# Seven-product matmuls whose running sums move from bank to bank of PSUM by ScalarE copies

## The chip, the core and the metric

The kernel runs on one core of a Trainium2 chip. The core has a matrix engine (TensorE, PE in the profile, with weight loads as PEld), a vector engine (VectorE, DVE), an activation engine (ScalarE, ACT), a general engine (GpSimd, POOL) and SyncE (SP), which issues most transfers. Matmul results go to PSUM, eight banks of 128 partitions by 512 fp32 values; everything else lies in SBUF. Each engine works through its own queue in order and waits on semaphores for the others. The metric is the device time of one execution in microseconds, from first to last instruction and what lies around them; lower is better.

## The reference, cut to what matters

The first part is a linear attention over 8 batches, 8 heads, 576 positions, 64 channels; its output becomes x of shape 4608 x 512. The change does not touch it. The second part routes all tokens through all eight experts, weighted:

```
x = attention output                      # (4608, 512)
P = sinkhorn(exp(x @ w_gate))             # (4608, 8), 8 rounds of normalising
for e in range(8):
    h = max(x @ w1[e], 0)                 # (4608, 512) @ (512, 1024)
    out += P[:, e:e+1] * (h @ w2[e])      # (4608, 1024) @ (1024, 512)
```

## The kernel before, in words

The tokens are cut into nine groups of 512 (group 8 holds the last 64 positions of each batch). Attention comes first, with expert 0's up matmuls filled in; routing and expert 0's down matmuls follow. From there on, experts 1 to 7 are computed with seven products in place of eight (a Strassen-Winograd scheme): both operands are seen as 2 x 2 blocks, VectorE makes sums and differences of blocks (`sub`, the line 1199 in the profile), and seven block products are combined into four result blocks.

*Up* (`up7`). One call treats two groups of 512 tokens at a time (pairs 0-1, 2-3, 4-5, 6-7, in two halves of the hidden width) or group 8 alone: nine calls per expert, 63 in all. In each call every product is made twice, for q = 0 and 1, each into a bank of its own. The products are named x1, x2, x3, x4, y1, w1, w2. The x products accumulate one after the other in bank x, w1 and w2 in bank w, y1 stands alone in bank y. Between them the running sum is read out:

- x1, then `keep`: ScalarE copies x to an SBUF tile U (line 1360). y1, then `add`: VectorE adds y and U, applies the relu and writes hidden block (1,1) (line 1364).
- x2 on top of x1, `keep` into a second U. x3 on top, `keep` into the first U; `add` of w (holding w1) and U gives block (0,0).
- x4 on top, `relu` by ScalarE (line 1369) gives block (0,1).
- w2 on top of w1, `add` of w and the second U gives block (1,0).

*Down* (`down7`) has the products X1, Y1, Z1, X2, X3, Z2, X4 of 8 matmuls each, in banks x, y and z, for one group of 512 tokens. `read` (line 1501) is two VectorE instructions that scale half a bank by the routing weight P and add it to the output accumulator. `read2` does the same by two ScalarE activations into an SBUF tile V (line 1513) and one GpSimd add onto the accumulator (line 1516). X1, Y1, Z1 and X3 end in `read2`, X2, Z2 and X4 in `read`. X1 and Y1 both belong to block (0,0) and are added to it one after the other. There are 62 such down sets.

Matmuls of 512 columns are line 1316 (`wide`, up of a pair), of 256 columns line 1307 (`product`, group 8's up and all downs). Each up set is issued together with the down set of an earlier group, in the order

`X1 x10 w10 x11 X2 x20 y10 x21 Z1 y11 X3 w11 x30 x31 x40 x41 w20 Y1 w21 X4 Z2`

where the digit at the end is q. This list is not yet the order on the chip. Every operation is handed to a planner (`Plan`), which keeps a cost for each operation, the dependencies, and the free PSUM banks (`Banks`, one shared set of eight; `P1` takes one bank, `P2` two). It lays the operations out in its own time: it always takes the one that can start first, on ties the one that comes earlier in the list, and emits each engine's instructions in that order. So a change of dependencies or of bank use moves the matmuls against each other. Expert weights are loaded by DMAs that GpSimd issues (line 476), the precombined blocks of x by DMAs from SyncE (line 1274). A matmul with `start=True` overwrites its bank, one with `start=False` adds to what stands there.

In the attention part VectorE also rewrites a bank in place between two sets of accumulating matmuls (line 872 between matmuls of line 864).

Of the kernel before, what the change touches and what calls it, by code (L numbers as in the profile page):

```python
# [69 lines left out]
class Banks:  # L70


    def __init__(self, tile, free, n):
        self.psum, self.free, self.n = True, free, n
        self.make = lambda i: tile[:, 512 * i:512 * (i + n)]

    def pick(self):

        if self.n == 1:
            order = sorted((t, i ^ 1 in self.free, i) for i, t in self.free.items())  # L80
            return (order[0][0], order[0][2]) if order else None
        order = sorted((max(self.free[i], self.free[i + 1]), i) for i in range(0, 8, 2)
                       if i in self.free and i + 1 in self.free)
        return order[0] if order else None

    def find(self, n):
        if n == 1:
            best = self.pick()
            return best and best[0]
        assert self.n == 1  # L90
        return sorted(self.free.values())[n - 1] if len(self.free) >= n else None

    def take(self, at):
        i = self.pick()[1]
        if self.n == 1:
            i = min((k ^ 1 in self.free, -t, -k, k) for k, t in self.free.items() if t <= at)[3]
        for k in range(self.n):
            del self.free[i + k]
        return i

    def give(self, end, slot):
# [215 lines left out]
def kernel(  # L317
# [11 lines left out]
    nc = tc.nc  # L329
# [130 lines left out]
    ring("s_p", [128, 3, E], FP32, "cs", 1)  # L460
    ring("s_p", [128, E], FP32, "c_bc", 1)
    banks = {i: 0.0 for i in range(8)}
    R["P1"], R["P2"] = Banks(ps, banks, 1), Banks(ps, banks, 2)

    def new(tag):
        return R[tag].new()
# [116 lines left out]
    def two(merged):  # L583

        if merged:
            b = new("P2")
            return [b], [lambda: b()[:, 0:512], lambda: b()[:, 512:1024]]
        b = [new("P1") for _ in range(2)]
        return b, b

    def tokens(pp, stat, n, r, takes=()):
# [35 lines left out]
    def rest_a(b, t):  # L627
# [4 lines left out]
        if b >= 2:  # L632
            rk = [(t["qk"], h, x) for h in range(2) for x in range(2)]
        if b < 2:
            ptr = new("P1")
            for pr in range(NP):
                pe(128, lambda pr=pr: nc.tensor.transpose(
                    ptr()[:, pr * 128:pr * 128 + 128],
                    acc[0][:, b, pr * 128:pr * 128 + 128], identf),
                    [("acc", 0, b, h, x) for h in range(2) for x in range(2)] + ["identf"],  # L640
                    [ptr, ("acc", 0, b)])
            dve(512, lambda: nc.vector.tensor_copy(
                out=rT().rearrange("p a b -> p (a b)"), in_=ptr()), [ptr], [rT])
        else:
            dma("SP", 1 << 17, 148, lambda: nc.sync.dma_start_transpose(
                out=rT(), in_=t["qk"]()[:, bi:bi + NP].rearrange("p a b c -> p (a b c)")),
                rk, [rT])
# [53 lines left out]
    def pair_a(b, pr, t):  # L701
# [3 lines left out]
        if b < 2:  # L705
            g = t["f"]
            for x in (1, 0):
                ptr = new("P1")
# [118 lines left out]
    def pair_b(b, pr, s, r):  # L827
# [4 lines left out]
        pkv = new("P1")  # L832

        def kvp(x):
            return pkv()[:, 0:4 * D1].rearrange("p (a b) -> p a b", a=2)[:, x, :]
# [18 lines left out]
        xb = new("xb")  # L854

        def outs(h):
            pn = new("P1")
# [27 lines left out]
    def pair_c(b, pr, xb):  # L885
        if b in (3, 4, 5, 6,):
# [4 lines left out]
        pxt = new("P1")  # L891
        for j in range(NJ):
            pe(128, lambda j=j: nc.tensor.transpose(  # L893
                bf(pxt)[:, j * 128:j * 128 + 128], xb()[:, j, :], ident),
# [3 lines left out]
            [pxt], [("xT", b, pr)])  # L898

    def rest_c(b, xbs):  # L900
        pxt = new("P1")
# [14 lines left out]
        return [("xTr", b, h) for b in range(B) for h in range(2)]  # L916

    def gate(g):
        pg = new("P1")
        for ti in range(4):  # L920
            for dc in range(NP):
                pe(8, lambda ti=ti, dc=dc: mm(
# [182 lines left out]
    def routing():  # L1105
        c_bc = None
        for it in range(8):
            rr, wv, cs, pc = new("rr"), new("T"), new("cs"), new("P1")
            lk = [("L", g) for g in range(NG)]
            if c_bc is None:  # L1110
                def u():
# [209 lines left out]
    def up7(A, gs, fp, X, H, r0):  # L1321


        pair = len(gs) == 2
# [5 lines left out]
                    "t4": (lambda: X[4](), [X[4]])}[n]  # L1330
            return f, r

        x, y, w = ([new("P1") for _ in range(2)] for _ in range(3))
        u = [[new("U") for _ in range(2)] for _ in range(2)]
        hb = [H[g][fp] for g in gs] if pair else H[gs[0]]

        def prod(bank, q, x, y, first, more=(), takes=(), wk=()):
# [18 lines left out]
        def okeys(q, i, j):  # L1356
            return [(z, q, i, j) for z in hb] if pair else [(hb[q], n, i, j) for n in range(2)]

        def keep(q, n):
            act(512, lambda: nc.scalar.copy(  # L1360
                out=u[q][n]().rearrange("p a b -> p (a b)"), in_=x[q]()), [x[q]], [u[q][n]])

        def add(bank, q, n, i, j):
            dve(515, lambda: nc.vector._custom_dve(  # L1364
                ADD_SAT, out=out_(q, i, j), in0=bank[q]().rearrange("p (a b) -> p a b", a=2),
                in1=u[q][n](), s0=3.0e38, s1=0.0), [bank[q], u[q][n]], okeys(q, i, j))

        def relu(q, i, j):
            act(512, lambda: nc.scalar.activation(  # L1369
                out=out_(q, i, j), in_=x[q]().rearrange("p (a b) -> p a b", a=2),  # L1370
                func=ACT.Relu, bias=0.0, scale=1.0), [x[q]], okeys(q, i, j))


        more = [("banks", 0), ("banks", 1)]
        more += [k for n in ("s2", "s3", "22") for k in A[n][1]] + [X[2]] + list(r0)

        def x1(q):
            prod(x, q, "11", "11", True, more, u[q] + hb)
            keep(q, 0)

        def y1(q):
            prod(y, q, "12", "21", True, r0, hb)
            add(y, q, 0, 1, 1)

        def x2(q):
            prod(x, q, "s2", "t2", False)
            keep(q, 1)

        def w1(q):
            prod(w, q, "s1", "t1", True, A["s4"][1] + r0, hb, [("banks", q)])  # L1390

        def x3(q):
            prod(x, q, "s3", "t3", False)
            keep(q, 0)
            add(w, q, 0, 0, 0)

        def x4(q):
            prod(x, q, "22", "t4", False)
            relu(q, 0, 1)

        def w2(q):
            prod(w, q, "s4", "22", False)
            add(w, q, 1, 1, 0)

        return {(n, q): lambda f=f, q=q: f(q) for n, f in (
            ("x1", x1), ("y1", y1), ("x2", x2), ("w1", w1), ("x3", x3), ("x4", x4), ("w2", w2))
# [5 lines left out]
    def down8(e, g, H, w2):  # L1412

        def tile_(ts, n0, n):
            py = new("P1")
# [25 lines left out]
    def down7(e, g, H, B7):  # L1441
# [79 lines left out]
        if e == 1 and g < 9:  # L1521
            for ts in range(4):
# [1 line left out]
                    out=acc[g][:, ts, :], in_=acc[g][:, ts, :], func=ACT.Copy, bias=0.0,  # L1524
                    scale=P[:, 4 * g + ts, 0:1]), ["P", ("acc", g, ts), (H[0], 0, 1, 1)] + akey(g),
                    [("acc", g, ts, j) for j in range(2)])
        x, y, z = new("P1"), new("P1"), new("P1")

        def X1():
            prod(x, a(0, 0), "11", hk(0, 0), True, sk(1) + hk(1, 0),  # L1530
                 [("D", e, g)])
            read2(x, 0, 0)

        def Y1():
            prod(y, a(0, 1), "21", hk(0, 1), True, [("D", e, g)])
            read2(y, 0, 0)

        def Z1():
# [116 lines left out]
```

## Time and profile before

| what | value |
|---|---|
| time, median of 3 runs (lowest, highest) | 1023.16 us (1022.22, 1023.96) |
| span of the profiled execution, first to last instruction | 1020.7 us |
| PE busy, matmuls | 1007.1 us (99%), 7944 |
| PEld busy | 686.1 us (67%) |
| DVE busy | 853.2 us (84%), 1833 instructions |
| ACT busy | 701.6 us (69%), 1530 instructions |
| POOL busy | 466.8 us (46%), 480 instructions |
| granted TensorE clock | 1.000 |
| chain that ended last | PE 95%, ACT 2%, DVE 1% |

The page gives no time of the profiled execution other than its span; the median of the runs is 2.5 us above that span.

How to read the lines that follow: a group line has the kernel line, the engine, the operation, output<-input by the program's names, the shapes, the count, then busy microseconds, mean nanoseconds of one, and the idle time of the engine just before these instructions with what ended it. A waits line reads "who <- for whom: us in total, times, longest". A timeline line reads start, duration, engine, line, operation and the number of instructions merged into it; a merged line covers from the first start to the last end. A matmul's recorded time includes its way through the array, so the spacing of starts, not the recorded duration, tells how dense TensorE is.

### The profile page before, as it was taken

The numbers are of one execution on the slowest core, as the hardware profiler recorded it, in microseconds if no ns is written. First come the engines' busy times: TensorE is split into PE (matmuls) and PEld (weight loads), VectorE is DVE, ScalarE is ACT, GpSimd is POOL, SyncE is SP. The second block draws the span as 40 slices with busy tenths as digits, with TensorE's granted clock in tenths as the row PEclk, the third lists the DMA queues.
The fourth block names the chain that finished last, engine by engine and source line by source line (L and its number), as shares of the span: only waits on it lengthen the run. The fifth ranks groups of instructions, "written<-read, shape, count | busy, mean of one in ns | idle before, by whom it ended". The sixth has DMA issues, their size and how long they took to land.

```text
span 1020.7 us, 21372 instructions
## 1 busy us (share of the span) xinstructions
PE 1007.1 (99%) x7944; PEld 686.1 (67%) x7944; DVE 853.2 (84%) x1833; ACT 701.6 (69%) x1530; POOL 466.8 (46%) x480
## 2 busy tenths in 40 slices
PE   7899999999999999999999999999999999999998
PEld 5666666644566766676667766676667666776665
DVE  7999989987888987788778887788778877888776
ACT  7999999836778665666666666556666666655663
POOL 5778764400244444444444444544444444544443
PEclk9999999999999999999999999999999999999999
DMA  9999988160103311161106111421125110612333
GB/s 264 174 194 175 174 149 126 36 114 11 42 32 69 82 32 32 27 135 32 32 27 114 33 42 37 82 54 32 31 47 115 32 32 26 109 43 73 129 124 130
DMA packets 107016, 82.86 MB, mean 81 GB/s; under 512 B 53536, under 2 KB 89376, under 8 KB 106912
## 3 DMA queue, kind: packets, MB, share of 16 engines
q1 hardware_dynamic: 74960, 57.44, 22.4%
q0 software_dynamic: 31648, 23.86, 16.9%
q8 instruction: 62, 1.02, 0.4%
q14 instruction: 42, 0.34, 0.1%
q10 hardware_dynamic: 304, 0.20, 0.1%
HBM read 83.18 MB, written 12.98 MB: 94 GB/s over the span
## 4 chain that ended last, share of the span: by engine, by line
PE 95%; ACT 2%; DVE 1%; issue 0%; POOL 0%; DMA 0%; DVEq 0%; ACTq 0%
PE ps L1307 41%; PE ps L1316 33%; PE ps L581 18%; PE ps L864 2%; PE ps L711 0%; ACT q L577 0%; DVE m L573 0%; ACT k L577 0%; DVE wx L573 0%; DMA acc<-in_k_dram 0%; PE ps L893 0%; ACT kr L577 0%; ACT wx L577 0%; DVE xb L878 0%; PE ps L903 0%
## 5 line engine op out<-in xcount | busy, mean ns | idle before, releaser
L1516 POOL TENSOR_TENSOR acc<-acc,hx 128x512 f32<-128x512 f32 x248 | 322.9, 1309 | 476.7 <-ACT hx L1513 473.3
L1360 ACT COPY U<-ps 128x512 f32<-128x512 f32 x378 | 216.6, 588 | 134.1 <-PE ps L1316 117.6
L1513 ACT ACTIVATE hx<-ps,P 128x256 f32<-128x256 f32 x496 | 208.0, 476 | 124.6 <-PE ps L1307 112.0
L1364 DVE CUSTOM_DVE_ANT_0 hs<-ps,U 128x512 bf16<-128x512 f32 x378 | 253.0, 687 | 35.7 <-PE ps L1316 15.0
L1307 PEld LDWEIGHTS <-hs 128*128 128x128 bf16 x1984 | 194.1, 98 | 72.8 <-issue 0.2
L1501 DVE SCALAR_TENSOR_TENSOR acc<-ps,P,acc 128x256 f32<-128x256 f32 x372 | 161.2, 478 | 92.3 <-PE ps L1307 91.5
L1307 PEld LDWEIGHTS <-hx 128*128 128x128 bf16 x1488 | 145.6, 98 | 40.0 <-issue 0.2
L1307 PE MATMUL ps<-hx,hs 128*128 128x256 bf16 x992 | 132.5, 273 | 0.0
L1316 PE MATMUL ps<-X,T 128*128 128x512 bf16 x448 | 129.0, 379 | 0.3 <-ACT U L1360 0.2
L1316 PE MATMUL ps<-xT,wx 128*128 128x512 bf16 x384 | 101.5, 379 | 0.0
L1316 PEld LDWEIGHTS <-T 128*128 128x128 bf16 x672 | 65.8, 98 | 48.0 <-issue 0.3
L1369 ACT ACTIVATE hs<-ps 128x512 bf16<-128x512 f32 x126 | 73.2, 609 | 12.3 <-PE ps L1316 12.3
L1307 PE MATMUL ps<-wx,hs 128*128 128x256 bf16 x560 | 80.4, 273 | 0.0
L1316 PEld LDWEIGHTS <-wx 128*128 128x128 bf16 x512 | 50.1, 98 | 38.4 <-issue 0.5
L1316 PE MATMUL ps<-xT,w 128*128 128x512 bf16 x288 | 75.6, 379 | 0.0
L581 PE MATMUL ps<-w,hx 128*128 128x512 bf16 x288 | 73.7, 379 | 0.0
L581 PE MATMUL ps<-xT,w 128*128 128x512 bf16 x288 | 72.9, 379 | 0.0
L1307 PE MATMUL ps<-wx,hx 128*128 128x256 bf16 x496 | 68.4, 273 | 0.0
L1316 PE MATMUL ps<-xT,T 128*128 128x512 bf16 x224 | 66.0, 379 | 0.0
L1307 PE MATMUL ps<-hx 128*128 128x256 bf16 x496 | 64.3, 273 | 0.1
L1199 DVE TENSOR_TENSOR hx<-hx,hs 128x512 bf16<-128x512 bf16 x124 | 64.2, 518 | 0.0
L1307 PE MATMUL ps<-w,hs 128*128 128x256 bf16 x432 | 62.7, 273 | 0.0
(147 smaller groups left out, 1516.2 us busy)
## 6 DMA issues: line engine op xcount, KB each, us to landing
X<-xd SPq DMA_DIRECT2D x72, 256.0 KB, 2.6
wx<-in_moe_w_dram POOLq DMA_DIRECT2D x8, 1024.0 KB, 12.5
v_m<-in_v_dram SPq DMA_DIRECT2D x15, 512.0 KB, 5.3
out_dram<-acc SPq DMA_DIRECT2D x14, 512.0 KB, 2.8
w<-in_moe_w_dram POOLq DMA_DIRECT2D x6, 1024.0 KB, 12.0
qk<-in_k_dram POOLq DMA_DIRECT2D x12, 256.0 KB, 5.5
qk<-in_q_dram POOLq DMA_DIRECT2D x12, 256.0 KB, 6.3
xd<-X SPq DMA_DIRECT2D x12, 256.0 KB, 2.1
```

The lines of the kernel that those rows point to most:

```text
L581: nc.tensor.matmul(out_, lhsT=lhsT, rhs=rhs, start=start, stop=stop)
L864: pe(65, lambda j=j: nc.tensor.matmul(pn()[:, j * D1:j * D1 + D1], lhsT=s["T"][x]()[:, j % 2, 2 * h + j // 2, :] if j < 4 else r["T"][x]() ...
L1199: lambda: f.tensor_tensor(out=out_(), in0=x(), in1=y(), op=op), r, w, **kw)
L1307: pe(256, lambda i=i, k=k, z=z: nc.tensor.matmul(bank()[:, 256 * i:256 * i + 256], lhsT=lhs(k, i), rhs=rhs(k), start=first and z, stop=k = ...
L1316: pe(512, lambda k=k: nc.tensor.matmul(bank().rearrange("p (a b) -> p a b", a=2), lhsT=lhs(k), rhs=rhs(k), start=first and k == 0, stop=k ...
L1360: act(512, lambda: nc.scalar.copy(out=u[q][n]().rearrange("p a b -> p (a b)"), in_=x[q]()), [x[q]], [u[q][n]])
L1364: dve(515, lambda: nc.vector._custom_dve(ADD_SAT, out=out_(q, i, j), in0=bank[q]().rearrange("p (a b) -> p a b", a=2), in1=u[q][n](), s0=3 ...
L1369: act(512, lambda: nc.scalar.activation(out=out_(q, i, j), in_=x[q]().rearrange("p (a b) -> p a b", a=2), func=ACT.Relu, bias=0.0, scale=1 ...
L1501: dve(320, lambda n=n, ts=ts: nc.vector.scalar_tensor_tensor(out=acc[g][:, ts, 256 * j:256 * j + 256], in0=bank()[:, 256 * n:256 * n + 256 ...
L1513: act(370, lambda n=n: nc.scalar.activation(out=u()[:, n, :], in_=bank()[:, 256 * n:256 * n + 256], func=ACT.Copy, bias=0.0, scale=P[:, 4 ...
L1516: pool(695, lambda: nc.gpsimd.tensor_tensor(out=acc[g][:, 2 * i:2 * i + 2, 256 * j:256 * j + 256], in0=acc[g][:, 2 * i:2 * i + 2, 256 * j: ...
```

## The change

In `up7` the running sums move inside PSUM. After x1, ScalarE copies bank x into bank y (`move`), and y1 accumulates on top of it, so bank y then holds the sum and ScalarE's relu writes block (1,1). After x2, ScalarE copies bank x into a new bank z, and w2 accumulates there. w1 is copied to U by ScalarE (`keep`) and its bank is given back. x3's sum in bank x and U are added by VectorE to block (0,0), and z and U to block (1,0). x4 is as before. Per q, ScalarE goes from three copies and one relu to three copies (two of them into PSUM) and two relus, VectorE from three adds to two.

In `down7`, X1 is copied by ScalarE from bank x to bank y, Y1 accumulates on top, and one `read2` takes the sum to block (0,0), where there were two.

The planner's banks get kinds: `whole` for a bank whose 512 columns are all written by the first matmuls, `part` for others, and `onto` for a bank that is first written by a copy; `onto` takes only banks whose last matmuls wrote all of it. `P1` is `whole`, the new `PP` is `part` (the attention, gate, routing and last down tiles use it), the new `PO` is `onto`. The order list is unchanged.

```diff
 class Banks:
+    def usable(self):
+        return [(i, t) for i, t in self.free.items() if self.kind != "onto" or i in self.whole]
...
         for k in range(self.n):
             del self.free[i + k]
+            (self.whole.discard if self.kind == "part" else self.whole.add)(i + k)
...
-    R["P1"], R["P2"] = Banks(ps, banks, 1), Banks(ps, banks, 2)
+    whole = set()
+    for tag, n, kind in (("P1", 1, "whole"), ("P2", 2, "part"), ("PP", 1, "part"),
+                         ("PO", 1, "onto")):
+        R[tag] = Banks(ps, banks, n, whole, kind)
...
-        x, y, w = ([new("P1") for _ in range(2)] for _ in range(3))
-        u = [[new("U") for _ in range(2)] for _ in range(2)]
+        x, w = ([new("PO" if q == 0 and t in inner else "P1") for q in range(2)]
+                for t in ("11", "s1"))
+        y, z = ([new("PO") for _ in range(2)] for _ in range(2))
+        u = [new("U") for _ in range(2)]
...
-        def keep(q, n):
+        def keep(q):
             act(512, lambda: nc.scalar.copy(
-                out=u[q][n]().rearrange("p a b -> p (a b)"), in_=x[q]()), [x[q]], [u[q][n]])
+                out=u[q]().rearrange("p a b -> p (a b)"), in_=w[q]()), [w[q]], [u[q]])
+        def move(to, q):
+            act(512, lambda: nc.scalar.copy(out=to[q](), in_=x[q]()), [x[q]], [to[q]])
...
         def x1(q):
-            keep(q, 0)
+            move(y, q)
         def y1(q):
-            prod(y, q, "12", "21", True, r0, hb)
-            add(y, q, 0, 1, 1)
+            prod(y, q, "12", "21", False, r0, hb)
+            relu(y, q, 1, 1)
         def x2(q):
             prod(x, q, "s2", "t2", False)
-            keep(q, 1)
+            move(z, q)
         def w1(q):
-            prod(w, q, "s1", "t1", True, A["s4"][1] + r0, hb, [("banks", q)])
+            prod(w, q, "s1", "t1", True, A["s4"][1] + r0, hb, [("banks", 0, q)])
+            keep(q)
         def x3(q):
             prod(x, q, "s3", "t3", False)
-            keep(q, 0)
-            add(w, q, 0, 0, 0)
+            add(x, q, 0, 0)
         def x4(q):
             prod(x, q, "22", "t4", False)
-            relu(q, 0, 1)
+            relu(x, q, 0, 1)
         def w2(q):
-            prod(w, q, "s4", "22", False)
-            add(w, q, 1, 1, 0)
+            prod(z, q, "s4", "22", False)
+            add(z, q, 1, 0)
...
-        x, y, z = new("P1"), new("P1"), new("P1")
+        x, y, z = new("P1"), new("PO"), new("P1")
         def X1():
-            read2(x, 0, 0)
+            act(512, lambda: nc.scalar.copy(out=y(), in_=x()), [x], [y])
         def Y1():
-            prod(y, a(0, 1), "21", hk(0, 1), True, [("D", e, g)])
+            prod(y, a(0, 1), "21", hk(0, 1), False, [("D", e, g)])
             read2(y, 0, 0)
```

More of the change, by code (lines that the diff above doesn't have):

```diff
@@ L70, with __init__ @@
 class Banks:
-    def __init__(self, tile, free, n):
+    def __init__(self, tile, free, n, whole, kind):
         self.psum, self.free, self.n = True, free, n
+        self.whole, self.kind = whole, kind
         self.make = lambda i: tile[:, 512 * i:512 * (i + n)]
+    def usable(self):
+        return [(i, t) for i, t in self.free.items() if self.kind != "onto" or i in self.whole]
     def pick(self):
         if self.n == 1:
-            order = sorted((t, i ^ 1 in self.free, i) for i, t in self.free.items())
+            order = sorted((t, i ^ 1 in self.free, i) for i, t in self.usable())
             return (order[0][0], order[0][2]) if order else None
@@ L90, in find @@
         assert self.n == 1
-        return sorted(self.free.values())[n - 1] if len(self.free) >= n else None
+        free = sorted(t for _, t in self.usable())
+        return free[n - 1] if len(free) >= n else None
     def take(self, at):
@@ L95, in take @@
         if self.n == 1:
-            i = min((k ^ 1 in self.free, -t, -k, k) for k, t in self.free.items() if t <= at)[3]
+            i = min((k ^ 1 in self.free, -t, -k, k) for k, t in self.usable() if t <= at)[3]
         for k in range(self.n):
             del self.free[i + k]
+            (self.whole.discard if self.kind == "part" else self.whole.add)(i + k)
         return i
@@ L587, in two @@
             return [b], [lambda: b()[:, 0:512], lambda: b()[:, 512:1024]]
-        b = [new("P1") for _ in range(2)]
+        b = [new("PP") for _ in range(2)]
         return b, b
@@ L634, in rest_a @@
         if b < 2:
-            ptr = new("P1")
+            ptr = new("PP")
             for pr in range(NP):
@@ L707, in pair_a @@
             for x in (1, 0):
-                ptr = new("P1")
+                ptr = new("PP")
                 i = 2 * x + h0 // 2
@@ L831, in pair_b @@
             [r["r"], (s["r"], 0)], [(s["r"], 1)])
-        pkv = new("P1")
+        pkv = new("PP")
         def kvp(x):
@@ L856, in outs @@
         def outs(h):
-            pn = new("P1")
+            pn = new("PP")
             def num():
@@ L890, in pair_c @@
             return
-        pxt = new("P1")
+        pxt = new("PP")
         for j in range(NJ):
@@ L900, in rest_c @@
     def rest_c(b, xbs):
-        pxt = new("P1")
+        pxt = new("PP")
         for pr in range(NP):
@@ L918, in gate @@
     def gate(g):
-        pg = new("P1")
+        pg = new("PP")
         for ti in range(4):
@@ L1107, in routing @@
         for it in range(8):
-            rr, wv, cs, pc = new("rr"), new("T"), new("cs"), new("P1")
+            rr, wv, cs, pc = new("rr"), new("T"), new("cs"), new("PP")
             lk = [("L", g) for g in range(NG)]
@@ L1319, in wide, with up7 @@
                 r, [bank, *(wk if k == 0 else ())], takes if k == 0 else ())
-    def up7(A, gs, fp, X, H, r0):
+    def up7(A, gs, fp, X, H, r0, inner=()):
         pair = len(gs) == 2
@@ L1357, in okeys @@
             return [(z, q, i, j) for z in hb] if pair else [(hb[q], n, i, j) for n in range(2)]
-        def keep(q, n):
+        def keep(q):
             act(512, lambda: nc.scalar.copy(
-                out=u[q][n]().rearrange("p a b -> p (a b)"), in_=x[q]()), [x[q]], [u[q][n]])
-        def add(bank, q, n, i, j):
+                out=u[q]().rearrange("p a b -> p (a b)"), in_=w[q]()), [w[q]], [u[q]])
+        def move(to, q):
+            act(512, lambda: nc.scalar.copy(out=to[q](), in_=x[q]()), [x[q]], [to[q]])
@@ L1364, in add, with relu @@
+        def add(bank, q, i, j):
             dve(515, lambda: nc.vector._custom_dve(
                 ADD_SAT, out=out_(q, i, j), in0=bank[q]().rearrange("p (a b) -> p a b", a=2),
-                in1=u[q][n](), s0=3.0e38, s1=0.0), [bank[q], u[q][n]], okeys(q, i, j))
-        def relu(q, i, j):
+                in1=u[q](), s0=3.0e38, s1=0.0), [bank[q], u[q]], okeys(q, i, j))
+        def relu(bank, q, i, j):
             act(512, lambda: nc.scalar.activation(
-                out=out_(q, i, j), in_=x[q]().rearrange("p (a b) -> p a b", a=2),
-                func=ACT.Relu, bias=0.0, scale=1.0), [x[q]], okeys(q, i, j))
@@ L1374, in up7 @@
-        more = [("banks", 0), ("banks", 1)]
+                out=out_(q, i, j), in_=bank[q]().rearrange("p (a b) -> p a b", a=2),
+                func=ACT.Relu, bias=0.0, scale=1.0), [bank[q]], okeys(q, i, j))
+        more = [("banks", i, q) for i in range(2) for q in range(2)]
         more += [k for n in ("s2", "s3", "22") for k in A[n][1]] + [X[2]] + list(r0)
         def x1(q):
-            prod(x, q, "11", "11", True, more, u[q] + hb)
-            keep(q, 0)
+            prod(x, q, "11", "11", True, more, u + hb)
+            move(y, q)
@@ L1414, in tile_ @@
         def tile_(ts, n0, n):
-            py = new("P1")
+            py = new("PP")
             for fc in range(8):
```

## The prediction, made before the result was known

> **What bounds the kernel now.** I read the page's busy table first, then the waits of TensorE, then windows and a timeline of the stage that the change touches. The span is 1020.7 us; the median of the runs, 1023.16, is 2.5 us above it. I sum against the span and add those 2.5 us back.
>
> ```profile
> span 1020.7 us, 21372 instructions
> ...
> PE 1007.1 (99%) x7944; PEld 686.1 (67%) x7944; DVE 853.2 (84%) x1833; ACT 701.6 (69%) x1530; POOL 466.8 (46%) x480
> ...
> 263.20:1017.00 753.80, 753.71 (x5408) 528.97 (x5407) 619.74 (x1298) 480.80 (x1011) 332.70 (x260) 1.00 0.25 60
> ...
> PE ps L1316 <- ACT U L1360: 0.2, 1, 0.2
> ```
>
> The third line is the window from 263.2 us to the last matmuls: its columns are length, then busy time of PE, PEld, DVE, ACT and POOL, then granted clock (1.00), DMA share and GB/s. PE is busy for 753.71 of 753.80 us. Matmul records overlap, so "busy" alone does not prove density; the starts do:
>
> ```profile
> 602.27 1.67 PE L1316 MATMUL ps<-xT,w 128*128 128x512 bf16 x7
> ...
> 612.68 1.04 PE L1307 MATMUL ps<-hx,hs 128*128 128x256 bf16 x8
> 613.56 1.04 PE L1307 MATMUL ps<-w,hx 128*128 128x256 bf16 x8
> 614.43 1.67 PE L1316 MATMUL ps<-xT,w 128*128 128x512 bf16 x7
> 615.94 0.59 PE L1316 MATMUL ps<-X,T 128*128 128x512 bf16 x2
> ...
> 261.88 1.03 PE L1316 MATMUL ps<-xT,wx 128*128 128x512 bf16 x4
> 263.14 0.38 PE L1316 MATMUL ps<-X,T 128*128 128x512 bf16 x1 [0.24 <-ACT U L1360]
> ...
> 262.51 0.59 ACT L1360 COPY U<-ps 128x512 f32<-128x512 f32 x1 [0.86 <-PE ps L1316]
> ```
>
> Eight narrow matmuls start in 0.88 us (0.109 each), seven wide ones in 1.51 us (0.216 each). A steady unit (one up product set with one down product set) has 28 wide and 56 narrow: 28 x 0.2158 + 56 x 0.1092 = 12.16 us, and the same block of seven starts at 602.27 and at 614.43: 12.16 us. Nothing is left between matmuls. After 250 us all gaps in the matmul starts of over 30 ns add up to 0.9 us, 0.6 of it at 263 to 265 us.
>
> The last three lines give the price of a round trip through ScalarE. The product ends with the matmul that starts at 262.09; the copy starts at 262.51, ends at 263.10, and the next matmul of that bank starts at 263.14. Its slot would have been 262.31: so a copy is hidden if 0.84 us of other matmuls stand between producer and user (0.20 handoff, 0.59 copy, 0.05 back). For a DVE add (687 ns) it is 0.94 us; for a read by two ScalarE activations (476 each, second start 0.36 after the first) 1.14 us.
>
> **The change, part by part.** The durations, from the page (out<-in, shapes, count | busy us, mean ns | idle before):
>
> ```profile
> L1516 POOL TENSOR_TENSOR acc<-acc,hx 128x512 f32<-128x512 f32 x248 | 322.9, 1309 | 476.7 <-ACT hx L1513 473.3
> L1360 ACT COPY U<-ps 128x512 f32<-128x512 f32 x378 | 216.6, 588 | 134.1 <-PE ps L1316 117.6
> L1513 ACT ACTIVATE hx<-ps,P 128x256 f32<-128x256 f32 x496 | 208.0, 476 | 124.6 <-PE ps L1307 112.0
> L1364 DVE CUSTOM_DVE_ANT_0 hs<-ps,U 128x512 bf16<-128x512 f32 x378 | 253.0, 687 | 35.7 <-PE ps L1316 15.0
> ...
> L1369 ACT ACTIVATE hs<-ps 128x512 bf16<-128x512 f32 x126 | 73.2, 609 | 12.3 <-PE ps L1316 12.3
> ```
>
> *Matmuls.* Their number, shapes and weights are the same, so the sum on the path is 0. The matmul order is the same up to the first seven-product set (238.5 us); from there on the planner orders anew. SP's queue keeps its order; POOL's 12 weight loads (12 us to landing) keep theirs with fewer adds ahead of them.
>
> *ScalarE.* 378 SBUF copies become 126 SBUF copies and 252 bank-to-bank copies; 126 relus become 252 (+126 x 609 ns = 77 us); 62 bank-to-bank copies come in the down sets (+62 x 588 = 36) and 124 activations of 476 go (-59). Net +54 us: 702 to 756, 74%. ScalarE then has 7.3 us of starts per 12.16 us unit. Not the bound.
>
> *VectorE and GpSimd.* 126 adds of 687 ns go (-87 us, 853 to 767), and 62 adds of 1309 ns (-81, 467 to 386). Both were off the path: 0.
>
> *What is gained.* Only the 0.9 us of gaps, and not surely.
>
> *The price of a bank-to-bank copy* is in no row. The same read with an SBUF write takes 588. From above: the slowest 128x512 ScalarE row (L1523, which reads SBUF) has 739. From below: 439, if a PSUM write saved as much as the PSUM read does (739-588). VectorE shows both destinations: PSUM to PSUM 495 for 325 elements (L872), PSUM to SBUF 486 for 320 (L878), 5 of the 9 ns being the elements. So the destination hardly matters; I take 588.
>
> *New waits.* I read the changed order of each queue from the built program and laid it on these durations. Smallest matmul time between producer and user over the 63 units, against the need:
> - first x product to y product, new copy: 1.40 us against 0.84; second x product to last w product (now on z): 2.16 against 0.84; X1 to Y1 in the down sets: 2.17 against 0.84.
> - X1 to X2: 0.98 against 0.84; before, 1.19 against 1.14. The margin grows from 0.05 to 0.14.
> - x1 to x2: 0.97 against 0.84, about as before.
> - x3 to x4: 0.98 (median 1.30) against 0.94. Before, a ScalarE copy freed the x bank in 0.84; now VectorE's add must, and behind it in VectorE's queue stand the w add and the subtractions.
>
> A wait on any of these holds all of PE, whose stream is in order. The queues in front count too. A steady unit starts its matmuls so (us; 8 narrow take 0.87, 2 wide 0.43): X1 0, x10 0.87, w10 1.30, x11 1.74, X2 2.17, x20 3.04, y10 3.47, x21 3.90, Z1 4.34, y11 5.21, X3 5.64, x30 6.51, w11 6.95, x31 7.38, w20 7.81, x40 8.02, Y1 8.67, x41 9.11, w21 9.98, X4 10.41, Z2 11.28. Tight are two places. The relu of y11 stands behind Z1's two reads (starts 5.47 and 5.83), runs 6.18 to 6.78 and must free a bank for w11 by 6.90: 0.12 to spare. The copy of w11 runs 7.58 to 8.16, the x31 add that needs it 8.20 to 8.88, x41's slot is 9.11: 0.18 to spare. In the first expert's units one wait of some 0.7 us (X4 behind X3's read) appears, while waits like the 0.6 us of before go. Sum: 0 to -0.9, and 0 to +0.7: 0. Span 1020.6, time 1023.0.
>
> *Banks.* The down y bank is held from X1's copy to Y1's read, near 10 us of 12; the w bank is given back after about 1 us rather than 8; laid out, the mean of banks held goes from 4.9 to 5.9 of 8. No matmul of a steady unit stands before its bank is free.
>
> *Seeding a bank from another engine.* The kernel already accumulates matmuls onto a bank that VectorE has rewritten: L872 (64 times) between the halves of L864, with one PE wait of 0.2 us behind it. The Trainium skill, "PSUM — Partial Sum Buffer", The four PSUM rules, speaks against the change: a seed written by ScalarE counts only where an earlier matmul left the element's written bit set, and any seed but 0 should rather go through TensorE. Followed so, 314 identity matmuls of 0.216 us would make the sum +68 us; the planner's new list of fully written banks meets the condition instead, at no matmul.
>
> **The rivals.**
>
> *A. VectorE held by GpSimd, ahead of x4 (slower).*
>
> ```profile
> 632.97 2.68 POOL L1516 TENSOR_TENSOR acc<-acc,hx 128x512 f32<-128x512 f32 x2 [3.08 <-ACT hx L1513]
> ...
> 633.18 1.34 DVE L1199 TENSOR_TENSOR hx<-hx,hs 128x512 bf16<-128x512 bf16 x1
> ...
> 314.55 2.80 POOL L1516 TENSOR_TENSOR acc<-acc,hx 128x512 f32<-128x512 f32 x2 [4.05 <-ACT hx L1513]
> ...
> 314.55 0.43 DVE L1199 TENSOR_TENSOR hx<-hs 128x512 bf16<-128x512 bf16 x1 [0.38 <-PE ps L1307]
> ```
>
> A subtraction that starts 0.21 us after a GpSimd add is held and takes 1.34 us in place of 0.42; one that starts together with it goes through, and the add waits. Before, this cost PE nothing. In the new order, in both halves of the first pair of experts 2 to 7, a subtraction stands between the x30 add and the x31 add. In the unit above: the x30 add starts at 7.15 and the subtraction 0.60 later, at 7.75; X3's second read ends at 7.61 and GpSimd's add starts 0.08 later, at 7.69. The gap is 0.06. If the subtraction is held it ends 0.28 after the add (as in the row), at 9.24, the x31 add at 9.84, and x41 starts at 9.89, not 9.11: 0.78 late, in 11 or 12 places: +9 us, 1032. It decides if the hold begins below 0.06 us. Against it: 0.06 is nearer to the 0.00 that went through than to 0.21. The Trainium skill, "SBUF — State Buffer", Who interferes with whom, has the same rule (two SBUF inputs contend with GpSimd's reads, and whoever issues first blocks the other); taken by issue order alone it would make the sum +9.
>
> *B. The bank-to-bank copy is slower than 588 (slower).* Up to about +0.1 us the covers hold; at the row's 0.74 us the tightest chain (0.97 against a need of 0.99), and what queues behind the copies, come up to 0.1 us late, once or twice in a unit, 70 times: +4, 1027.
>
> *C. Banks short.* If y11's relu slips by over 0.12 us behind the reads, w11 finds no bank: slipping 0.2, 63 x 0.08 = +5, 1028. Against it: ScalarE has 4.8 of 12.16 us free in the unit.
>
> *D. Faster.* The floor is matmul starts plus the first 238 us, both unchanged: at most 0.9 us, 1022.2. Beyond 0.2% there is nothing to win.
>
> **How the numbers follow.** 0.2% is about 2 us, what a measurement of this kernel can tell. Forecast (no change) 0.78; A 0.10; B 0.06; C 0.04; a gain over 2 us 0.02. The forecast alone gives 1021.6 to 1024.8; the range takes in B's 1027 and leaves most of A and C (0.14) and some run-to-run scatter below out: 1021.4 to 1027.5. Faster 0.02, same 0.78, slower 0.20.
>
> **What would show it.** Right: PE without waits from about 270 us, starts still 0.109 and 0.216, ScalarE near 756 us, VectorE 767, GpSimd 386, the new copy at 560 to 600 ns. A shows as x4 matmuls that wait for a VectorE add, behind subtractions of 1.3 us or more at one place per unit; B as a copy row of over 0.7 us and waits at x2; C as w matmuls that wait for ScalarE. The prediction is wrong if PE shows repeated waits in each unit, or if matmul starts spread while ScalarE writes to PSUM.

## The result, and the profile after

The changed kernel takes 1032.66 us (median of 4 runs, 1032.15 to 1033.41), against 1023.28 us (1022.22 to 1023.96) for the kernel before on the same chip: a ratio of 1.0096, 95% interval 1.0081 to 1.011. It is slower by 9.4 us; "no change" was forecast. The profiled spans differ by 9.5 us, 1030.2 against 1020.7, so the profile holds the whole loss.

The head of the page of the changed kernel:

```profile
span 1030.2 us, 21214 instructions
...
PE 1008.4 (98%) x7944; PEld 685.3 (67%) x7944; DVE 786.1 (76%) x1707; ACT 745.0 (72%) x1594; POOL 380.0 (37%) x418
```

VectorE and GpSimd have less to do than before, as the diff says, the number of matmuls is the same and TensorE's busy time grew by 1.3 us only. So the other 8 us must be waits. The waits of TensorE (who <- for whom: total, times, longest):

```profile
PE ps L1326 <- DVE hs L1379: 7.8, 10, 0.8
PE ps L721 <- DMA acc<-in_k_dram: 4.0, 1, 4.0
...
PE ps L1317 <- ACT hx L1528: 0.6, 1, 0.6
```

The first line is new: ten waits of a 512-column matmul for VectorE's add (line 1379, line 1364 before). The second lies in the attention part and is no part of the change. The view counts from the recorded end of the matmul before; a gap in the starts is some 0.17 us longer for each wait. The gaps over 30 ns in the matmul starts after 230 us give the ledger:

| gaps in the matmul starts after 230 us | before | after |
|---|---|---|
| four of 0.85 us and six of 1.01 us, each ahead of an x41 matmul | 0 | 9.46 |
| X4 behind X3's read in the first expert, at 273.72 us | 0 | 0.75 |
| everything else | 0.9 | 0.45 |
| sum | 0.9 | 10.66 |

The difference, 9.8 us, is the 9.5 us of the spans to within 0.3 us. One of the ten places, in the timeline of the changed kernel (start, duration, engine, line; in brackets the idle time before and its releaser):

```profile
465.41 0.69 DVE L1379 CUSTOM_DVE_ANT_0 hs<-ps,U 128x512 bf16<-128x512 f32 x1 [0.96 <-PE ps L1326]
...
465.91 1.27 POOL L1531 TENSOR_TENSOR acc<-acc,hx 128x512 f32<-128x512 f32 x1
...
466.02 1.45 DVE L1209 TENSOR_TENSOR hx<-hx,hs 128x512 bf16<-128x512 bf16 x1
...
467.39 1.27 DVE L1379 CUSTOM_DVE_ANT_0 hs<-ps,U 128x512 bf16<-128x512 f32 x2
468.12 0.38 PE L1326 MATMUL ps<-X,wx 128*128 128x512 bf16 x1 [0.69 <-DVE hs L1379]
```

This is rival A, link by link. The x30 add starts at 465.41. GpSimd's add of X3's product starts at 465.91. A subtraction follows the x30 add in VectorE's queue at 466.02, about 0.1 us after GpSimd's add; it takes 1.45 us in place of 0.42 and ends 0.29 us after GpSimd's add does. The x31 add waits behind it until 467.39, ends near 468.07, and x41 starts at 468.12. The matmuls before x41 leave its slot at 467.27: 0.85 us late. In the six waits of 1.01 us the subtraction has 1024 columns and takes 1.72 us in place of 0.69.

Over the window from 263.2 us to the last matmuls (length, busy of PE, PEld, DVE, ACT and POOL, clock, DMA share, GB/s) TensorE is no longer full: 754.41 us of 762.80, at an unchanged clock of 1.00. The matmuls themselves did not slow down.

```profile
263.20:1026.00 762.80, 754.41 (x5402) 528.29 (x5401) 555.03 (x1176) 521.08 (x1070) 246.01 (x198) 1.00 0.25 59
```

The same run also holds a place without the wait, in expert 5, with the same instructions in the same queues:

```profile
688.20 0.69 DVE L1379 CUSTOM_DVE_ANT_0 hs<-ps,U 128x512 bf16<-128x512 f32 x1 [0.96 <-PE ps L1326]
...
688.81 0.41 DVE L1209 TENSOR_TENSOR hx<-hx,hs 128x512 bf16<-128x512 bf16 x1
...
688.99 1.36 POOL L1531 TENSOR_TENSOR acc<-acc,hx 128x512 f32<-128x512 f32 x1 [0.39 <-POOL acc L1531]
689.14 1.37 DVE L1379 CUSTOM_DVE_ANT_0 hs<-ps,U 128x512 bf16<-128x512 f32 x2
...
690.06 0.59 PE L1326 MATMUL ps<-X,wx 128*128 128x512 bf16 x2
```

Here GpSimd's add happens to start 0.18 us after the subtraction. The subtraction takes 0.41 us, the x31 add starts 0.33 us after it, and x41 waits for nothing. Why this one GpSimd add started late the records do not tell.

### The profile page after: what moved, and what is told of

It reads as the page before. It is cut to its first block, busy times and chain, and to the rows that moved or that the text cites. A ratio compares the mean times of both kernels' runs of the same rounds, so it can differ in the third digit from the quotient of the medians.

```text
span 1030.2 us, 21214 instructions
## 1 busy us (share of the span) xinstructions
PE 1008.4 (98%) x7944; PEld 685.3 (67%) x7944; DVE 786.1 (76%) x1707; ACT 745.0 (72%) x1594; POOL 380.0 (37%) x418
## 4 chain that ended last, share of the span: by engine, by line
PE 92%; DVE 3%; ACT 2%; issue 2%; DMA 1%; SPq 0%; DVEq 0%; ACTq 0%
PE ps L1317 41%; PE ps L1326 31%; PE ps L591 18%; PE ps L874 2%; DVE hs L1379 1%; DMA acc<-in_q_dram 1%; ACT k L587 1%; ACT q L587 1%; DVE m L583 0%; DVE wx L583 0%; PE ps L721 0%; PE ps L903 0%; ACT kr L587 0%; ACT wx L587 0%; DVE ps L882 0%
## 5 line engine op out<-in xcount | busy, mean ns | idle before, releaser
L1531 POOL TENSOR_TENSOR acc<-acc,hx 128x512 f32<-128x512 f32 x186 | 236.2, 1270 | 573.1 <-ACT hx L1528 569.2
L1379 DVE CUSTOM_DVE_ANT_0 hs<-ps,U 128x512 bf16<-128x512 f32 x252 | 169.4, 686 | 51.9 <-PE ps L1326 35.3
L1376 ACT COPY ps<-ps 128x512 f32<-128x512 f32 x252 | 144.0, 587 | 77.9 <-PE ps L1326 65.9
L1384 ACT ACTIVATE hs<-ps 128x512 bf16<-128x512 f32 x252 | 151.5, 605 | 54.4 <-PE ps L1326 48.0
L1528 ACT ACTIVATE hx<-ps,P 128x256 f32<-128x256 f32 x372 | 156.3, 473 | 46.4 <-PE ps L1317 44.9
L1326 PE MATMUL ps<-X,T 128*128 128x512 bf16 x448 | 132.8, 379 | 0.0
L1209 DVE TENSOR_TENSOR hx<-hs 128x512 bf16<-128x512 bf16 x124 | 50.4, 420 | 42.6 <-PE ps L1317 27.3
L1372 ACT COPY U<-ps 128x512 f32<-128x512 f32 x126 | 74.7, 593 | 4.0 <-PE ps L1326 3.9
L1547 ACT COPY ps<-ps 128x512 f32<-128x512 f32 x62 | 35.7, 575 | 57.8 <-PE ps L1317 45.0
L1317 PE MATMUL ps<-wx,hs 128*128 128x256 bf16 x560 | 75.8, 273 | 0.0
L1326 PE MATMUL ps<-xT,T 128*128 128x512 bf16 x224 | 74.9, 379 | 0.0
```

Of the source, the lines that this page charges most:

```text
L1209: lambda: f.tensor_tensor(out=out_(), in0=x(), in1=y(), op=op), r, w, **kw)
L1317: pe(256, lambda i=i, k=k, z=z: nc.tensor.matmul(bank()[:, 256 * i:256 * i + 256], lhsT=lhs(k, i), rhs=rhs(k), start=first and z, stop=k = ...
L1326: pe(512, lambda k=k: nc.tensor.matmul(bank().rearrange("p (a b) -> p a b", a=2), lhsT=lhs(k), rhs=rhs(k), start=first and k == 0, stop=k ...
L1372: act(512, lambda: nc.scalar.copy(out=u[q]().rearrange("p a b -> p (a b)"), in_=w[q]()), [w[q]], [u[q]])
L1376: act(512, lambda: nc.scalar.copy(out=to[q](), in_=x[q]()), [x[q]], [to[q]])
L1379: dve(515, lambda: nc.vector._custom_dve(ADD_SAT, out=out_(q, i, j), in0=bank[q]().rearrange("p (a b) -> p a b", a=2), in1=u[q](), s0=3.0e ...
```

## The experiments

The theory after the result: TensorE's ten waits come from VectorE's subtraction, which starts just after GpSimd's add, is held by it, and stands in the queue ahead of the x31 add that frees x's bank. The rivals: the hold is a coincidence and x4 is late because VectorE's add rather than a ScalarE copy frees the bank; or the pressure on banks or on ScalarE does it.

**Only the order of VectorE's queue.** Where a lone subtraction stands between the x30 add and the x31 add, it is issued after the x31 add, in 18 places. Nothing else is touched; the same instructions run.

```diff
         done = self.schedule()
+        for i in [n for n, o in enumerate(done) if o.mark == "x30"]:
+            a, b = [j for j in range(i + 1, len(done)) if done[j].eng == "DVE"][:2]
+            if done[a].shared and done[b].mark == "x31":
+                done.insert(b, done.pop(a))
...
         def add(bank, q, i, j):
...
+            if bank is x:
+                plan.ops[-1].mark = f"x3{q}"
```

> The changed kernel; only in VectorE's queue, wherever one subtraction stands alone between the x30 add and the x31 add, it is issued after the x31 add (18 places, 10 of them those with a wait). Nothing else moves. Theory A (the subtraction is held by the GpSimd add and the x31 add stands behind it): the ten waits of x41 go (9.5 us), 1023.2 us, within 1 us. Rival 'VectorE in the x chain' (the 687 ns add and its handoffs are too long for x4's cover by themselves): the add still starts no earlier than the copy of w11 allows, and most of the loss stays, 1030 or more. Rival 'the hold matters wherever it falls': the moved subtraction is still held, the w20 add behind it comes late, and half or more of the loss stays, 1028 or more.

Measured: 1024.21 us (10 runs, 1023.07 to 1025.08) against 1022.71 us (31 runs) before, ratio 1.0014 (1.0004 to 1.0023); profiled span 1021.0. The ten waits are gone, and the gaps after 230 us add up to 1.87 us, 0.76 of it the wait in the first expert and 0.42 a single wait for an x31 add at 672.19 us with no held subtraction ahead of it. The median is 1.5 us over the kernel before, just past the 1 us that was allowed for. The profiled execution is the fastest of the ten (1023.07 us), so its profile does not show where the rest goes. The place that was shown, in this kernel's timeline (line 1384 is the add, 1214 the subtraction, 1538 GpSimd's add):

```profile
462.20 2.64 POOL L1538 TENSOR_TENSOR acc<-acc,hx 128x512 f32<-128x512 f32 x2 [6.12 <-ACT hx L1535]
...
464.01 0.69 DVE L1384 CUSTOM_DVE_ANT_0 hs<-ps,U 128x512 bf16<-128x512 f32 x1 [0.26 <-ACT U L1377]
...
464.62 0.50 DVE L1214 TENSOR_TENSOR hx<-hx,hs 128x512 bf16<-128x512 bf16 x1
...
464.92 0.59 PE L1331 MATMUL ps<-X,wx 128*128 128x512 bf16 x2
```

GpSimd's second add runs until 464.84 (the merged line of two). The x31 add, which takes one operand from PSUM and one from SBUF, runs beside it in its usual 0.69 us as soon as ScalarE's copy U is there; x41 follows without a wait. So freeing the bank by VectorE is not the cause by itself: moving the subtraction back by one place in its queue gives back 8 of the 9.4 us. Both rivals named above fall. The moved subtraction is still held, but only for the last 0.2 us of GpSimd's add (0.50 us in place of 0.41), so this run says little about a long hold in a place that nobody waits for; the kernel with the up part alone, below, has such holds.

**Only the time at which GpSimd starts.** A copy of two columns on GpSimd ahead of each add of X3's product makes that add start later. GpSimd has 62 instructions more, and VectorE's order stays that of the changed kernel.

```diff
+            def add():
+                if late:
+                    nc.gpsimd.tensor_copy(out=tiny, in_=u()[:, 1, 0:2])
+                nc.gpsimd.tensor_tensor(
...
         def X3():
             prod(x, a(1, 0), "t3", hk(1, 0), False)
-            read2(x, 1, 1)
+            read2(x, 1, 1, True)
```

> The changed kernel; GpSimd copies two columns of V to a spare tile ahead of every add of X3's product, so that this add starts some 0.15 to 0.25 us later; planner and all other queues are as in the changed kernel. GpSimd gets more work, not less. Theory A: the subtraction now starts before the add, keeps the port, and the waits of x41 shrink from 0.85 and 1.01 us to 0.2 or less, since the small copy itself may hold the subtraction for its own time of about 0.2: 1023 to 1025 us. Rival 'VectorE in the x chain': nothing changes, 1032. Rival 'GpSimd as such is late': GpSimd's adds end later than before, so the time rises over 1033.

Measured: 1023.50 us (10 runs, 1022.75 to 1025.4), ratio 1.0012 (1.0002 to 1.0021). The gaps after 230 us are 1.21 us, none for VectorE's adds. (The profiled execution has a 1.4 us wait in the attention part that the change does not touch.) The timeline:

```profile
466.87 0.19 POOL L1535 COPY tiny<-hx 128x2 f32<-128x2 f32 x1
...
466.98 0.41 DVE L1210 TENSOR_TENSOR hx<-hx,hs 128x512 bf16<-128x512 bf16 x1
467.01 1.52 POOL L1536 TENSOR_TENSOR acc<-acc,hx 128x512 f32<-128x512 f32 x1
...
467.32 1.37 DVE L1380 CUSTOM_DVE_ANT_0 hs<-ps,U 128x512 bf16<-128x512 f32 x2
```

Now the subtraction starts 0.03 us before GpSimd's add. It goes through in 0.41 us, and the add is stretched by 0.25 us, from 1.27 to 1.52, which nobody waits for. GpSimd has more work than in the changed kernel and the kernel is more than 8 us faster: the load does not matter, the order of two starts does.

**The two halves of the change.** One kernel has the up part alone (`down7` as before), the other the down part alone (`up7` as before).

```diff
-        x, y, z = new("P1"), new("PO"), new("P1")
+        x, y, z = new("P1"), new("P1"), new("P1")
...
-            act(512, lambda: nc.scalar.copy(out=y(), in_=x()), [x], [y])
+            read2(x, 0, 0)
...
-            prod(y, a(0, 1), "21", hk(0, 1), False, [("D", e, g)])
+            prod(y, a(0, 1), "21", hk(0, 1), True, [("D", e, g)])
```

> Only the up part of the change: the down sets read X1 and Y1 by two reads as in the kernel before, on a bank each. The planner orders anew. Theory A (a meeting of two queues in the combined order, not the bank copies or the VectorE add in the chain): in this order no lone subtraction meets a GpSimd add ahead of x41, so 1023 to 1025 us with no wait that repeats. Rival 'VectorE in the x chain': this part alone has it in all 126 chains, so 1030 or more. Rival 'the down part costs it': 1023.

The down part alone, the core of its diff:

```diff
         def x1(q):
-            prod(x, q, "11", "11", True, more, u + hb)
-            move(y, q)
+            prod(x, q, "11", "11", True, more, u[q] + hb)
+            keep(q, 0)
...
         def x3(q):
             prod(x, q, "s3", "t3", False)
-            add(x, q, 0, 0)
+            keep(q, 0)
+            add(w, q, 0, 0, 0)
```

> Only the down part: X1 copied to Y1's bank, one read less; the up sets as in the kernel before. Theory A: no repeated wait in the order that the planner makes here, 1022.5 to 1024.5 us. Rival 'the down part costs it' (the y bank held for 10 us, or X1's copy late): 1030 or more, with waits of X2 or of w.

Measured: up alone 1024.74 us (10 runs, 1023.91 to 1025.08), ratio 1.0016 (1.0007 to 1.0026); down alone 1023.07 us (10 runs, 1022.74 to 1024.03), ratio 1.0002 (0.9993 to 1.0012). Neither has the repeated wait. In the stages that the change touches one line grows, that of the single wait behind X3's read, in the waits of the kernel with the up part alone:

```profile
PE ps L1317 <- ACT hx L1528: 1.1, 1, 1.1
```

So neither half costs the 9 us; it takes the two together. With the down part alone, ScalarE's copy still frees x's bank, and x4 waits for no VectorE add. With the up part alone, the adds are on TensorE's path but the planner's order is another: in the first pair of experts 2 to 7 either no subtraction or a run of five stands between the x30 and the x31 add. Six subtractions are held there too (they start 0.05 to 0.12 us after a GpSimd add and take 1.49 to 1.75 us), and cost TensorE nothing: none of them stands ahead of an x31 add that TensorE waits for.

**A shorter hold.** The add of X3's product is made by two GpSimd adds of half the size.

```diff
+            def add():
+                for c in range(2) if parts == 2 else (slice(0, 2),):
+                    t = slice(2 * i + c, 2 * i + c + 1) if parts == 2 else slice(2 * i, 2 * i + 2)
+                    nc.gpsimd.tensor_tensor(
...
         def X3():
             prod(x, a(1, 0), "t3", hk(1, 0), False)
-            read2(x, 1, 1)
+            read2(x, 1, 1, 2)
```

> The changed kernel; the GpSimd add of X3's product is issued as two adds of half the columns. Its start stays, 0.10 us before the subtraction; the first half should run about 0.7 us where the whole runs 1.27. Theory A (the subtraction is held until the GpSimd instruction that runs ends): the hold is 0.6 us shorter, the waits of x41 fall from 0.85 and 1.01 us to about 0.25 and 0.4, so the loss from 9.5 to about 3.5 us: 1026 us. Rival 'the subtraction waits for all of GpSimd's queue': the waits stay or grow with the second half's start-up, 1032 to 1034. Rival 'the loss isn't the hold': 1032.

Measured: 1026.97 us (5 runs, 1026.2 to 1027.84), ratio 1.0037 (1.0024 to 1.005): a loss of 3.95 us against the kernel before on the same chip, where about 3.5 was expected. The timeline of the same place, and the line of its waits of TensorE:

```profile
465.95 1.59 POOL L1535 TENSOR_TENSOR acc<-acc,hx 128x256 f32<-128x256 f32 x2
466.07 0.89 DVE L1209 TENSOR_TENSOR hx<-hx,hs 128x512 bf16<-128x512 bf16 x1
...
467.62 0.59 PE L1326 MATMUL ps<-X,wx 128*128 128x512 bf16 x2
```

```profile
PE ps L1326 <- DVE hs L1379: 1.7, 6, 0.3
```

The first half takes 0.73 us. The subtraction starts 0.12 us after it and takes 0.89 us: it ends 0.28 us after the end of the first half, as it ended 0.29 after the whole add in the changed kernel. The second half does not stop it. The gaps ahead of x41 are five of 0.29 us and six of 0.45 us, 4.2 us in all, in place of 9.46. (The waits view counts six of them, from the recorded end of the matmul before.) So the loss goes with the length of the GpSimd instruction that is running when the subtraction starts. Expert 5's first place is among the eleven here.

**How small a lead is enough.** A two-column ScalarE copy between X3's two reads lets GpSimd's add start 0.06 us later in relation to the subtraction, which brings the lead of 0.1 us below the 0.06 us that the prediction had worked out.

```diff
+                def half(n=n):
+                    if late and n:
+                        nc.scalar.copy(out=tiny, in_=bank()[:, 0:2])
+                    nc.scalar.activation(
```

> The changed kernel; ScalarE copies two columns of X3's bank between its two reads, so that GpSimd's add of X3's product starts 0.06 to 0.10 us later and the gap between it and the subtraction shrinks from 0.10 to 0.00 to 0.04 us. Theory 'whoever starts first holds the other': held as before while the gap is above 0, 1031 to 1033 us, or free where it falls to 0 or below. Theory 'a subtraction less than some 0.05 us late still gets through', by which the forecast took the gap of 0.06 for harmless: 1023 to 1024.5 us at a gap of 0.02 to 0.04.

Measured: 1033.89 us (4 runs, 1033.5 to 1035.59), ratio 1.011 (1.0093 to 1.0127) against 1023.02 us (8 runs) before; this is 0.9 us over the upper end of the 1031 to 1033 us that was expected of a hold. The timeline:

```profile
467.04 1.26 POOL L1537 TENSOR_TENSOR acc<-acc,hx 128x512 f32<-128x512 f32 x1 [0.16 <-ACT hx L1532]
467.08 1.51 DVE L1210 TENSOR_TENSOR hx<-hx,hs 128x512 bf16<-128x512 bf16 x1
...
469.24 0.38 PE L1327 MATMUL ps<-X,wx 128*128 128x512 bf16 x1 [0.75 <-DVE hs L1380]
```

With a lead of only 0.04 us GpSimd still holds the subtraction for its whole length, and all ten waits are there, 0.06 us longer each (four of 0.91, six of 1.07): the later GpSimd's add starts while it still comes first, the later everything behind it ends. One row for each kind of meeting, by how long after GpSimd's add the subtraction starts:

| subtraction starts after GpSimd's add by | GpSimd's add takes | a 512-column subtraction takes |
|---|---|---|
| -0.18 (the changed kernel, expert 5) | 1.36 | 0.41 |
| -0.03 (GpSimd later) | 1.52 | 0.41 |
| 0.00 (before, 314.55 us) | 2.80 for two in a row | 0.43 |
| 0.04 (ScalarE's small copy) | 1.26 | 1.51 |
| 0.10 to 0.11 (the changed kernel) | 1.27 | 1.45 |
| 0.12 (half adds) | 0.73 | 0.89 |
| 0.21 (before, 633.18 us) | 2.68 for two in a row | 1.34 |

There is no middle in these rows: the one that starts first runs, the other is held. One case goes both ways. Where GpSimd's add starts while VectorE is already in a subtraction, the next subtraction behind that one was held at five places of the kernel with the up part alone (it starts 0.12 us after the add; 460.18 us is the first), but went through at two places of the kernel before (267.84 and 897.19 us, 0.13 and 0.24 us after the add). What decides there was not tried; ahead of x41 VectorE comes from the x30 add, not from a subtraction.

## Why the prediction was wrong, point by point

- *TensorE is dense, and nothing but a new wait can move the time.* Right. The number of matmuls, their spacing and the clock are unchanged, and the ten waits with the one behind X3's read are the whole difference to within 0.3 us.
- *The price of a bank-to-bank copy.* Right: 588 ns was taken, and the changed kernel's groups show 587 and 575 (the third line is the copy to SBUF):

```profile
L1376 ACT COPY ps<-ps 128x512 f32<-128x512 f32 x252 | 144.0, 587 | 77.9 <-PE ps L1326 65.9
...
L1547 ACT COPY ps<-ps 128x512 f32<-128x512 f32 x62 | 35.7, 575 | 57.8 <-PE ps L1317 45.0
...
L1372 ACT COPY U<-ps 128x512 f32<-128x512 f32 x126 | 74.7, 593 | 4.0 <-PE ps L1326 3.9
```

  Rival B is out: no matmul waits for these copies.
- *Seeding a bank from another engine costs no matmul.* Right: 7944 matmuls before and after, and 314 banks are seeded by ScalarE. The +68 us that the rule of the Trainium skill, "PSUM — Partial Sum Buffer", The four PSUM rules, would have meant if followed by identity matmuls did not have to be paid. The planner gives these copies only banks that earlier matmuls have written in full, the condition under which that page lets a seed count; no run here tries a bank without it.
- *Banks and the relu of y11 (rival C).* No repeated wait of w11 for ScalarE appears.
- *One wait of 0.7 us in the first expert.* Right in place and size: 0.75 us at 273.72 us, ahead of X4, in the timeline of the changed kernel:

```profile
273.72 1.03 PE L1317 MATMUL ps<-hx,hs 128*128 128x256 bf16 x8 [0.58 <-ACT hx L1528]
```

- *The busy sums.* ScalarE came to 745.0 (756 forecast), VectorE to 786.1 (767), GpSimd to 380.0 (386). The two larger misses come mostly from one way of counting: busy time is counted once where two records overlap, and instructions that follow each other overlap by about 0.1 us. An add of 687 ns starts 0.598 us after the one before it. So 126 adds fewer are worth 75 us, not 87, which gives 778; the kernels without the holds at x31 have 777.7 and 777.0, and the holds bring the changed one to 786.1. ScalarE's relus, copies and activations start 0.50, 0.48 and 0.37 us apart when they follow each other, which gives 748 instead of 756. Neither engine was the bound, so this moved no term of the sum.
- *Rival A, which is what happened.* Mechanism and place were as worked out, count and price nearly so: twelve places, of which expert 7's second has no subtraction between the adds and expert 5's first went free, leaves ten; each 0.85 or 1.01 us where 0.78 had been taken; 9.46 us in place of 9. The larger price has two reasons. GpSimd's add starts 1.36 us ahead of x41's slot (465.91 against 467.27) rather than the 1.42 that was worked out (7.69 against 9.11), and everything behind it comes that much later. And in six of the ten places the subtraction has 1024 columns, so that a longer rest of it runs after GpSimd is done. The first of these was left out of the working: GpSimd's start was taken from ScalarE's read alone, which ends at 465.77, but the add before it in GpSimd's own queue ends at 465.82, and this one starts 0.09 us later. The two, in the timeline of the changed kernel (the first line holds both GpSimd adds):

```profile
464.55 2.64 POOL L1531 TENSOR_TENSOR acc<-acc,hx 128x512 f32<-128x512 f32 x2 [6.12 <-ACT hx L1528]
...
464.93 0.84 ACT L1528 ACTIVATE hx<-ps,P 128x256 f32<-128x256 f32 x2
```

**The step that failed** is the weighing: "Against it: 0.06 is nearer to the 0.00 that went through than to 0.21." By it the wait of x41, which the prediction had priced at +9 us, went into the sum as nothing; it measured 9.46 us. Two things were wrong with it. The gap itself is some 0.1 us, so the estimate of 0.06 was off by most of its own size: against x41's slot GpSimd's add came 0.06 us and the subtraction 0.11 us later than worked out. A difference between two starts, each at the end of its own chain of durations, was not to be had to 0.06 us here. And the distance says nothing: even the 0.06 us as worked out would have been held, since 0.04 was. The two rows of the trace of before, 0.00 and 0.21, were not two ends of a scale between which a value can be placed; they were two outcomes of one question, who starts first. The rule of the Trainium skill, "SBUF — State Buffer", Who interferes with whom, that whoever issues first blocks the other, said that, and taken by itself would have given the +9 us. The measured table agrees with it down to 0.04 us. With the lead worked out on GpSimd's side, as it then was in ten of the eleven places that have such a subtraction, the chance of A should have been well over a half, not 0.10.

The two things that made this possible were also both in the prediction, but not put together with a weight: the tight place ("0.18 to spare" at x41) and a subtraction that now stands in front of it. Before, the 13 subtractions that were held for 1.34 us cost nothing: a ScalarE copy freed x's bank, as it still does with the down part alone. In the changed kernel, too, there are 21 other held subtractions (0.93 to 1.01 us) and TensorE waits behind none of them; 13 of them even stand ahead of an x31 add, but there VectorE is idle again before that add can start (from 405.51 to 406.01 us in the first). The change did not create the hold; it put an add that TensorE waits for behind one.

The planner could not show this. It marks VectorE's subtractions and GpSimd's adds as `shared` and never lets two of them overlap in its own time, so in its plan the two never meet; on the chip the order of each queue is kept but not the planner's times, and the two start 0.10 us apart.

## What to carry to other kernels

In a stream that one engine fills without gaps, an instruction that is newly put on that engine's path brings its neighbours in the queue with it: list what stands ahead of it, and ask of each not what it takes on average but the longest it takes anywhere in the trace. Where two engines share something that the first to start keeps for a whole instruction, a lead worked out as small is not a small risk; count it as lost unless the order is made certain, and price it by the whole instruction. Making it certain was cheap here: the changed kernel came within 0.2% of the kernel before by a swap of two instructions in VectorE's queue (in 18 places), or by a copy of two columns on an engine that is idle 60% of the time.

## What the hardware showed that had not been expected

- A delay that pays: each of the small GpSimd copies takes 0.19 us, moves the add behind it by some 0.13 us in relation to the subtraction, and saves 0.85 or 1.01 us at ten places. A delay of 0.06 us by way of ScalarE, which did not change who comes first, saved nothing (1033.89 us).
- The order is settled within 0.04 us: at -0.03 VectorE went through, at 0.04 GpSimd held it for its full 1.26 us.
- A held 512-column subtraction ends 0.28 to 0.29 us after the GpSimd instruction that holds it, whether that took 0.73 or 1.27 us, which is less than the 0.41 us that it takes when free. Whether a part of it runs before the hold takes effect was not tried. With 1024 columns it ends 0.55 us after. The second of two back-to-back GpSimd adds did not hold again a subtraction that the first had held.
- A ScalarE copy of 128x512 fp32 from PSUM takes the same time into PSUM (587 and 575 ns) as into SBUF (593 ns here, 588 before).
